# Segment 0's x turned by DMA transposes instead of TensorE, and half of wq on ScalarE's DMA queue

## The chip, the core and the metric

The kernel runs on one core of a Trainium2 chip. A core has TensorE (matmuls, output into PSUM), VectorE, ScalarE, GpSimd, SyncE (which here only issues DMAs) and 16 DMA engines. The engines run side by side, each through its own list of instructions in order, and wait for one another by semaphores. In the profile they are PE (PEld for TensorE's weight loads), DVE, ACT, POOL and SP. The metric is the device time of one execution in microseconds (us). The kernel before takes 264.84 us (median of 3 runs, 264.73 to 264.94).

## The reference

The input is x (2048 tokens by 512, bfloat16). Two branches read it, and a gate per token mixes them:

```python
g = sigmoid((x * gate_w).sum(-1, keepdims=True))
a = attention(x, wq, wk, wv, wo, beta)      # 32 heads of 16, 4 segments of 512 tokens
b = (relu(x @ W_gate) * (x @ W_up)) @ W_down  # inner width 1792
out = g * a + (1 - g) * b
```

In the attention each segment of 512 tokens has causal softmax attention within itself, and from segment 1 on a recall from a running memory `M` (16 x 16 a head) and normaliser `z` that sum phi(k) v and phi(k) over earlier segments; sigmoid(beta) mixes the two a head, and wo projects the result.

## The kernel before

**Tiling.** The work goes segment by segment (`NSEG = 4`, `L = 512` tokens). Every projection needs x with its features on the partitions: `xT[seg % 3]` is 128 x 4 x 512, block `ci` holding features 128 ci to 128 ci + 127 of the segment's 512 tokens. A projection of 128 outputs is four matmuls of 512 columns, one for each `ci`, summed in one of PSUM's 8 banks. Heads come in four groups (`c`) of eight; a group's q goes to `QT`, its k through `ktr` to `KT` with masks. Scores (`qk`, line 616, and `qk_diag`, line 629) fill four banks, ScalarE takes their exponent (line 638), and the values follow (`pv`, line 689). The FFN (`ffn_tasks`) runs over 14 inner tiles with `wg_sb` and `wu_sb`, then `wd_sb` and `wo_sb` for the output (`out_tile`).

**The order of the work.** Nothing is scheduled when the program is built: each piece is a task (`plan.add`) with an engine and dependencies, and the string `ORDER` lists all tasks by number in the order in which they are issued. `UNITS` gives each task its buffers. `LANDS` is the planner's estimate, in nanoseconds, of when each load arrives. Matmul tasks may run as one 128-column matmul (line 461) or as four 32-column ones (line 465), so that TensorE's array needs no change of mode; scores use it by rows, values by columns.

**The start.** All weights and segment 0's x are loaded at the start, from SyncE's queue but for three loads from ScalarE's (lines 300 to 327). Segment 0's x is loaded as it stands, tokens on the partitions, into `xn`, in four pieces: columns 0 to 255 of tokens 0 to 255 (`n0`, SyncE) and 256 to 511 (`n1`, ScalarE), then columns 256 to 511 likewise (`n2`, `n3`). Between them go wq's first two row blocks (`q0`, `q1`), after them wq's other half (`qb`), wk in two halves, wv, and the first pieces of the FFN weights. Meanwhile TensorE heats (`heat`, line 904): seven matmuls on constants, six of 512 columns and one of 384. Then `x0_tasks` turns x by matmuls against an identity (`flip`, line 498): 16 of 128 columns, two to a PSUM bank, each pair copied to `xT[0]` by VectorE (tokens 0 to 255) or ScalarE (256 to 511) (line 511). After the first eight turns a matmul on zeros (`junk`, line 505) fills the wait for the copies. Four projections by `wq` come between the first and the second eight turns. `proj_q` for segment 0 takes `ci` 0 and 1 as tasks of their own, and `ci` 2 and 3 as a third.

The same `xn` serves the token gate: `gate_tasks` multiplies it with `gwb` on VectorE (line 415) and sums. `xT` of segments 1 to 3 is not turned by TensorE: a DMA transpose brings each from x (`load_xT`, line 273); phi(k) is turned by DMA transposes too (`pK`, line 581). A DMA reports to its semaphore once from each of the 16 DMA engines, and has landed with the sixteenth report; the trace records the time of each report, and the text calls them its reports or landing records. Loads share eight semaphores in turn.

Of the kernel before, what the change touches and what calls it, by code (L numbers as in the profile page):

```python
# [12 lines left out]
P = 128  # L13
S = 2048
D = 512
# [15 lines left out]
    0 1 2 3 4 5 6 7 8 9 10 11 12 13 14 15 16 17 18 19 20 21 22 23 24 27 28 30 32 29 34 31 33 35  # L31
    36 83 57 70 84 37 43 41 39 38 58 44 96 42 40 97 71 59 85 60 98 61 86 62 99 74 63 87 72 64
    67 75 66 65 88 73 123 76 109 124 112 68 110 78 214 77 113 111 80 215 125 89 114 126 217 216
    81 220 127 91 218 47 115 116 90 46 223 93 129 128 219 25 224 130 221 117 238 26 239 226 222
    132 240 227 229 133 131 225 230 118 92 94 119 244 79 228 45 135 120 419 134 231 136 245 420
    48 241 121 242 421 49 416 122 246 147 243 365 50 148 137 232 346 55 233 69 51 138 366 53
    235 367 234 82 417 52 150 368 371 139 369 54 677 418 151 140 141 236 149 247 142 360 95 237
    152 153 361 143 154 248 56 362 256 250 249 257 144 363 350 100 258 156 145 251 157 259 364
    425 372 260 426 349 252 101 373 427 167 158 261 253 168 102 422 155 374 146 423 103 375 104
    106 424 262 169 170 376 159 171 107 263 160 161 108 254 347 393 264 172 255 173 377 394 174  # L40
    162 265 379 395 268 348 266 399 269 163 175 267 176 270 286 164 105 177 280 400 380 378 281
    401 388 381 389 282 178 179 385 390 289 180 271 382 384 287 397 165 283 284 370 166 290 288
    285 391 194 191 195 291 272 192 274 181 275 193 292 276 197 398 351 183 182 198 184 196 273
    293 185 295 186 296 352 294 199 200 354 356 187 407 297 201 357 550 188 408 396 189 551 402
    409 552 403 202 190 413 203 430 355 404 277 204 278 358 412 411 298 414 1008 299 556 431
    279 405 205 449 310 432 450 415 544 545 392 311 410 312 386 557 546 300 558 433 452 387 383
    206 353 453 406 207 434 301 208 451 302 209 313 454 455 210 696 456 428 303 314 429 304 359
    305 211 212 440 697 457 458 441 213 315 316 459 698 306 747 699 700 748 701 307 702 749 460
    461 317 308 462 753 703 318 309 750 704 751 754 463 752 474 755 334 475 335 464 336 756 319
    337 320 476 477 465 478 321 757 467 338 322 466 758 479 339 468 480 323 481 469 324 691 470  # L50
    471 692 325 472 553 482 693 483 340 484 559 326 554 341 555 694 560 485 495 561 327 547 496
    695 548 328 549 586 329 497 498 486 499 330 488 331 587 332 487 588 500 501 333 489 435 568
    502 436 569 490 437 342 571 491 572 438 570 492 504 439 607 503 573 505 608 493 580 343 583
    344 581 506 507 582 345 584 442 508 604 585 605 443 589 574 575 606 510 523 576 520 509 524
    590 609 577 591 578 511 521 579 525 526 512 513 527 562 522 592 514 563 610 515 564 528 529
    611 530 516 595 517 613 614 518 593 612 596 531 594 532 615 565 533 597 601 622 623 566 624
    598 534 567 599 625 600 780 535 781 602 537 616 617 603 536 618 782 783 538 619 784 626 759
    620 539 627 875 1072 760 876 540 621 785 444 877 1069 446 1073 445 1070 881 1074 1071 1075
    448 705 1076 447 706 1077 494 676 786 519 710 707 787 711 473 1027 541 1028 640 712 708 641
    788 542 642 716 882 1029 789 883 709 628 790 1022 1030 629 1032 714 1066 715 713 630 717  # L60
    1023 792 543 631 718 791 1024 793 1067 643 679 644 680 632 1025 633 1068 805 645 646 806
    795 647 794 634 1031 635 681 648 719 678 649 1026 808 796 809 650 807 636 637 798 651 797
    682 638 724 683 810 799 811 685 652 812 687 639 800 738 684 688 653 654 739 655 740 813 814
    725 815 686 741 656 742 726 664 689 657 743 720 727 665 729 744 728 658 721 816 730 905 745
    722 666 906 731 826 746 907 908 827 690 909 723 878 732 667 801 910 879 668 802 659 828 880
    829 817 803 830 887 819 888 660 818 889 831 669 820 832 893 833 821 670 822 894 823 661 824
    733 895 671 834 662 734 835 663 735 896 836 897 672 898 673 890 674 736 891 837 838 892 675
    929 839 930 737 911 920 912 931 884 840 913 885 841 921 854 886 761 932 855 762 933 763 917
    918 934 842 919 764 856 857 765 844 766 899 858 922 900 914 767 843 768 915 901 859 845 860
    902 916 861 903 771 769 923 846 904 924 772 944 847 770 925 848 953 863 862 849 926 864 941  # L70
    927 942 928 945 943 954 865 935 946 955 1099 866 1100 947 868 938 936 774 939 937 773 1101
    1102 867 940 1103 956 869 957 950 1079 1197 958 1104 775 870 948 776 1198 949 777 951 1199
    1038 804 1060 952 1191 779 1192 1061 778 1193 1055 871 1062 1007 1105 1039 850 1106 1033
    1065 1063 1034 1064 825 1056 1040 1203 1035 1204 1107 1108 1057 1205 1044 1043 1109 971
    1041 872 959 972 1042 873 960 961 1058 1078 973 1111 1036 874 962 1059 1112 963 974 1012
    964 965 1009 975 1114 1124 966 1011 1125 976 977 1037 978 979 1010 1045 1113 1127 851 1013
    1128 1046 1110 967 852 980 1126 968 981 1115 1014 1047 1129 1116 969 1016 1130 1117 982 983
    970 1131 1015 995 1018 1118 996 1019 984 1048 985 997 1049 1119 1132 1017 998 853 1133 1050
    1134 1206 1051 1020 999 1000 986 1054 1052 987 1053 1135 1145 1001 1146 1200 1021 1207 1120
    1121 1201 1002 1208 988 1147 1122 1148 1136 1149 1202 1003 1138 1004 1137 1005 989 1150  # L80
    1139 1151 1006 1080 1194 1152 1140 1221 1081 1141 1082 1209 1222 1142 990 1223 1154 1083
    1143 1153 1195 1084 1155 991 1196 1224 992 1210 993 1227 1156 1211 1157 994 1225 1158 1218
    1226 1090 1219 1228 1091 1212 1229 1230 1159 1170 1160 1085 1213 1171 1086 1231 1214 1215
    1216 1232 1239 1087 1217 1172 1173 1161 1174 1220 1240 1163 1162 1233 1088 1164 1234 1089
    1241 1175 1176 1165 1235 1236 1166 1177 1242 1167 1245 1168 1254 1246 1243 1178 1247 1179
    1092 1244 1237 1180 1093 1255 1238 1248 1249 1251 1250 1252 1181 1272 1253 1094 1182 1256
    1257 1095 1269 1184 1258 1263 1123 1259 1270 1096 1260 1271 1097 1183 1144 1266 1169 1267
    1185 1261 1275 1098 1287 1186 1273 1262 1276 1187 1274 1288 1264 1188 1289 1277 1265 1189
    1278 1279 1268 1290 1190 1280 1281 1291 1282 1292 1283 1293 1284 1294 1285 1295 1296 1286
    1299 1297 1300 1301 1302 1298 1311 1303 1304 1312 1305 1306 1313 1307 1314 1308 1315 1316  # L90
    1309 1317 1318 1319 1320 1310 1323 1324 1321 1325 1326 1327 1328 1329 1330 1331 1322 1334
    1335 1332 1336 1337 1338 1339 1333 1340 1341 1342 1343 1344 1345
"""

UNITS = (
    "456701230123437651300021111002224122032230000012000000020011000002000020000230111030011120"
    "02103432331105303722061118021a012d110b2039301c00111200112003013223002101312012022210110456"
    "1032000002200000002201100000130000000011011212202203031001930232127312532362238322b0014110"
    "a302d010c120110013221000110013220033101123323302145670321000002000000003301100000300003000"
    "0110113221211520132222122820302037110911243226210a120b320d302c0012120132321221212000322713"  # L100
    "30013456023100000230000000320110000020000000070011100311223231313002182225002410263107323a"
    "0119007c314d122b10011200110"
)


class Slot:


    def __init__(self, cands):
        self.cands, self.units, self.left = tuple(cands), (), 0  # L110

    @property
# [66 lines left out]
def kernel(  # L179
# [74 lines left out]
    def work():  # L254
        return plan.one("ps", range(7, -1, -1))


    LANDS = dict(n0=3700, n1=3750, n2=6000, n3=6050, q0=4950, q1=4950, qb=6800, ka=7900, kb=9300,
                 v=11500, g0=13000, u0=14000, gw=14800, be=15100, g1=16300, u1=17500, x1=20700,
                 g2=22000, u2=23100, g3=24200, u3=25300, d0=28100, d1=30800, o=33600)  # L260

# [708 lines left out]
```

## Time and profile before

| what | value |
|---|---|
| median of 3 runs | 264.84 us (264.73 to 264.94) |
| the profiled execution | 264.77 us |
| its span, first to last instruction | 263.1 us |
| TensorE (PE) busy | 259.0 us, 98% |
| VectorE (DVE) busy | 205.0 us, 78% |
| ScalarE (ACT) busy | 184.2 us, 70% |
| GpSimd (POOL) busy | 63.3 us, 24% |
| share of the DMA engines' time, queue 1 (SyncE) and queue 10 (ScalarE) | 25.3%, 0.5% |

Times in the profile are us from the span's start. A timeline line has the start, the duration of the group, the engine (`SPq` is SyncE's instruction queue issuing a DMA), the line of the kernel, the operation, what it writes and reads, and how many; in square brackets the engine's idle time before it and what ended it. A line of the waits has who waited for whom, the total in us, how often, and the longest. A line of the chain has start, duration and what ran: it is followed back from the last instruction to what released each step. A line of the windows has the stretch, its length, each engine's busy time in it, TensorE's granted clock, the DMA engines' busy share and GB/s. The clock column reads 1.00 throughout this trace, also where the spacing of the matmuls shows half speed; the text goes by the spacing. A busy TensorE includes the pipeline's latency, so the distance from one matmul's start to the next tells more than the busy share.

### The profile page before, as it was taken

The page shows a single profiled execution, that of the slowest core. Times are in us where ns is not written, and L with a number is a line of the kernel's source. Part 1 is how long each engine was busy: PE and PEld are TensorE (multiplying, and loading weights), DVE is VectorE, ACT ScalarE, POOL GpSimd, SP SyncE. Part 2 cuts the span into 40 slices and gives each one's busy share as a digit, 9 for nine tenths or more (in the row PEclk, how much of TensorE's full clock was granted, in tenths as well). Part 3 has the DMA queues.
Part 4 walks back from the last instruction along what each step waited for, and adds up shares of the span by engine and source line. Part 5 has one row for each costly group of instructions (what it writes and reads, how often), then busy time and mean ns, then how long its engine had stood idle before and what let it go on. Part 6 is the DMA issues. An engine that isn't in the chain of part 4 may idle for free.

```text
span 263.1 us, 8894 instructions
## 1 busy us (share of the span) xinstructions
PE 259.0 (98%) x3854; PEld 118.6 (45%) x3854; DVE 205.0 (78%) x474; ACT 184.2 (70%) x170; POOL 63.3 (24%) x168
## 2 busy tenths in 40 slices
PE   8999999999999999999999999999999999999995
PEld 3444434454444454544444444444444444445454
DVE  2899999899985666856999778794998887868622
ACT  3299988999777678887675877778487667892000
POOL 8022623223321323132012222032131223121000
DMA  6999892100822001200210120023020200320011
GB/s 199 328 273 346 231 187 42 24 2 18 132 82 60 2 22 36 79 2 2 80 22 22 36 42 21 22 75 110 0 82 1 57 5 30 102 73 22 2 42 42
DMA packets 30526, 19.46 MB, mean 74 GB/s; under 512 B 15000, under 2 KB 28952, under 8 KB 30488
## 3 DMA queue, kind: packets, MB, share of 16 engines
q1 hardware_dynamic: 29800, 18.51, 25.3%
q8 instruction: 30, 0.49, 0.8%
q10 hardware_dynamic: 688, 0.39, 0.5%
q14 instruction: 8, 0.07, 0.1%
HBM read 13.21 MB, written 2.55 MB: 60 GB/s over the span
## 4 chain that ended last, share of the span: by engine, by line
PE 92%; DVE 6%; issue 0%; DVEq 0%
PE ps L461 52%; PE ps L465 21%; PE ps L616 8%; PE ps L689 7%; PE ps L904 1%; PE ps L629 1%; DVE QT L549 1%; DVE KT L568 1%; DVE ktr L565 1%; PE ps L809 1%; DVE gcat L392 1%; PE ps L498 1%; PE ps L745 1%; DVE junk L415 0%; DVE hT L859 0%
## 5 line engine op out<-in xcount | busy, mean ns | idle before, releaser
L638 ACT ACTIVATE E<-ps 128x2048 bf16<-128x2048 f32 x64 | 120.1, 1877 | 33.2 <-PE ps L616 25.0
L667 POOL TENSOR_SCALAR_AFFINE_SELECT E<-E 128x256 bf16<-128x256 bf16 x128 | 54.0, 447 | 169.2 <-ACT E L638 169.2
L859 DVE TENSOR_TENSOR hT<-ps,rgr 128x512 bf16<-128x512 f32 x56 | 37.8, 680 | 15.0 <-PE ps L461 10.3
L853 ACT ACTIVATE rgr<-ps 128x512 bf16<-128x512 f32 x56 | 33.0, 597 | 15.7 <-PE ps L461 8.7
L461 PE MATMUL ps<-xT,wu_sb 128*128 128x512 bf16 x162 | 43.8, 380 | 0.0
L461 PE MATMUL ps<-wd_sb,hT 128*128 128x512 bf16 (+1 forms) x176 | 40.7, 354 | 0.0
L461 PE MATMUL ps<-xT,wg_sb 128*128 128x512 bf16 x146 | 40.1, 380 | 0.0
L720 DVE STREAM_TRANSPOSE T<-ps 128x512 f32<-128x512 f32 x32 | 22.4, 708 | 9.5 <-PE ps L689 9.2
L616 PE MATMUL ps<-QT,KT 32*128 32x320 bf16 (+3 forms) x512 | 25.4, 273 | 0.0
L461 PEld LDWEIGHTS <-wu_sb 128*128 128x128 bf16 x162 | 14.6, 98 | 18.1 <-issue 2.7
L461 PEld LDWEIGHTS <-hT 128*128 128x128 bf16 x176 | 15.0, 98 | 17.0 <-issue 2.7
L885 DVE TENSOR_SCALAR osr<-ps,ngcol 128x512 bf16<-128x512 f32 (+2 forms) x18 | 12.3, 687 | 12.6 <-PE ps L465 8.5
L461 PEld LDWEIGHTS <-wg_sb 128*128 128x128 bf16 x146 | 13.7, 98 | 16.9 <-issue 1.3
L465 PE MATMUL ps<-xT,wg_sb 128*32 128x512 bf16 x312 | 20.3, 379 | 0.0
L689 PE MATMUL ps<-E,Vp 128*17 128x320 bf16 (+3 forms) x512 | 19.4, 273 | 0.0
L616 PEld LDWEIGHTS <-KT 32*128 32x128 bf16 x512 | 7.6, 92 | 24.9 <-issue 22.5
L465 PE MATMUL ps<-wd_sb,hT 128*32 128x512 bf16 (+1 forms) x304 | 17.5, 359 | 0.0
L461 PE MATMUL ps<-xT,wq_sb 128*128 128x512 bf16 x62 | 17.5, 391 | 0.0
L461 PE MATMUL ps<-wv_sb,xT 128*128 128x512 bf16 x62 | 17.0, 379 | 0.0
L638 ACT ACTIVATE Em<-ps 128x2048 bf16<-128x2048 f32 x8 | 15.0, 1876 | 2.6 <-PE ps L629 2.6
L465 PE MATMUL ps<-xT,wu_sb 128*32 128x512 bf16 x248 | 16.7, 379 | 0.0
L461 PE MATMUL ps<-xT,wk_sb 128*128 128x512 bf16 x60 | 16.6, 380 | 0.0
(102 smaller groups left out, 301.0 us busy)
## 6 DMA issues: line engine op xcount, KB each, us to landing
out_dram<-osr SPq DMA_DIRECT2D x15, 128.0 KB
wd_sb<-in_B_W_down_dram SPq DMA_DIRECT2D x2, 896.0 KB
xn<-in_A_x_dram SPq DMA_DIRECT2D x3, 512.0 KB
cdr<-coefs SPq DMA_DIRECT2D x6, 256.0 KB
xn<-coefs SPq DMA_DIRECT2D x6, 256.0 KB
wg_sb<-in_B_W_gate_dram SPq DMA_DIRECT2D x2, 512.0 KB
wu_sb<-in_B_W_up_dram SPq DMA_DIRECT2D x2, 512.0 KB
wg_sb<-in_B_W_gate_dram SPq DMA_DIRECT2D x2, 384.0 KB
```

What stands on the lines that cost most here:

```text
L392: nc.vector.tensor_copy(gcat[rows, 0, c], g[rows, 0, c, (m + c) % 4])
L461: nc.tensor.matmul(out, lhsT=lhsT, rhs=rhs, start=start, stop=stop)
L465: nc.tensor.matmul(out[r], lhsT=lhsT[:, r], rhs=rhs, start=start, stop=stop, tile_position=(0, 32 * j))
L498: nc.tensor.matmul(bank(sl)[:, k * P:(k + 1) * P], lhsT=xn[:, 2 * t + k, ci * P:(ci + 1) * P], rhs=ident[:], start=True, stop=True)
L616: nc.tensor.matmul(ps[:, j * L + o:j * L + o + L - q], lhsT=KT[i][rows, kb, 3 * r:3 * r + 2].rearrange("p h q -> p (h q)"), rhs=QT[i][rows ...
L638: last_exp[0] = [plan.add("ACT", 66 + 4 * L / 1.2, key, lambda: nc.scalar.activation(dst, ps[:, 0:4 * L], ACT.Exp, scale=SCALE), [a] + war ...
L667: nc.gpsimd.affine_select(out=m[:, :, o:o + HP], in_=m[:, :, o:o + HP], compare_op=ALU.is_ge, fill=0.0, base=HP, pattern=[[0, 4], [1, HP]] ...
L689: nc.tensor.matmul(bank(sl)[32 * m:32 * m + HW, q:q + w], lhsT=(Vp[i] if n < 4 else Vm)[:, kb, r, 4 * c + j, 0:HW], rhs=rhs, start=(n == 0 ...
L720: done.append(plan.add("DVE", 633, key - RL, lambda r=r, sl=sl: nc.vector.transpose(T[ts.i][:, r], bank(sl)), [a] + done, 75 if r else 0, ...
L853: r = plan.add("ACT", 478, key - RL, lambda sl=gsl, rs=rs: nc.scalar.activation(rgr[rs.i][:], bank(sl), ACT.Relu), [g], ACL, frees=[gsl])
L859: nc.vector.tensor_tensor(hT[hs1.i][:], bank(sl), rgr[rs.i][:], ALU.mult)),
L885: nc.vector.tensor_scalar(osr[os.i][:, n0 - c0:n1 - c0], bank(sl)[:, 0:n1 - n0], ngcol[:, tt:tt + 1], None, ALU.mult)),
```

## The change

Segment 0's x is turned by TensorE for its first 128 columns only: two loads (`n0`, `n1`) bring those, 64 KB each instead of 128, four turns and one copy on VectorE and one on ScalarE follow. Two DMA transposes on SyncE's queue, in its third and fourth place, bring the other three blocks of `xT[0]` straight from x: one of 128 columns (`xb`), one of 256 (`x0`). wq's second half (`qb`) goes to ScalarE's queue, as its third load. Since `xn` still serves the token gate, its other 384 columns are loaded later, after the second pieces of the FFN weights and before segment 1's transpose (`n2`). The heating loses its last matmul of 384 columns; the filler on zeros becomes two of 256 columns. `LANDS`, `ORDER` and `UNITS` are new throughout: the order of all tasks of the program is another one.

```diff
-    LANDS = dict(n0=3700, n1=3750, n2=6000, n3=6050, q0=4950, q1=4950, qb=6800, ka=7900, kb=9300,
+    LANDS = dict(n0=3360, n1=3400, q0=4450, q1=4650, xb=5300, x0=6500, qb=6700, ka=7900, kb=9300,
...
-    got_n[0] = [load_x0(eng, 0, t) for t, eng in enumerate((nc.sync, nc.scalar))]
+    first, rest = slice(0, P), slice(P, D)
+    got_n[0] = [load_x0(eng, 2 * t, 2 * t + 2, first, "n%d" % t)
+                for t, eng in enumerate((nc.sync, nc.scalar))]
     got_q = [load(eng, wq_sb[:, ci, :], A_wq[ci * P:(ci + 1) * P, :], "q%d" % ci)
              for ci, eng in enumerate((nc.sync, nc.scalar))]
-    got_n[0] += [load_x0(eng, 1, t) for t, eng in enumerate((nc.sync, nc.scalar))]
-    got_q.append(load_rows(nc.sync, wq_sb, A_wq, 1, "q"))
+    got_x0b = []
+    for a, b, n in ((1, 2, "xb"), (2, NC, "x0")):
+        nc.sync.dma_start_transpose(out=xT[0][:, a:b, :], in_=x[0:L, a * P:b * P])
+        got_x0b.append(arrival(n))
+    got_q.append(load_rows(nc.scalar, wq_sb, A_wq, 1, "q"))
...
     load_gu(1)
+    got_n[0].append(load_x0(nc.sync, 0, NC, rest, "n2"))
     load_xT(1)
...
     def x0_tasks():
         got = []
-        for ci in range(NC):
-            for t in range(2):
+        for t in range(2):
...
+        def idle():
+            for k in range(2):
+                nc.tensor.matmul(bank(js)[:, 0:2 * P], lhsT=junk[:, 0:P],
+                                 rhs=junk[:, None, 0:P].to_broadcast([P, 2, P]), start=True,
+                                 stop=True)
+        j = plan.add("PE", 428, K(-9) + 2, idle, [a], lat=0, need=[js], frees=[js], size=4)
+        x0_first.extend([got + [(j, 0.0)], [got_x0b[0]]])
+        return [got + [got_x0b[0]], [got_x0b[1]]]
...
-        for k in range(7):
-            w = L if k < 6 else 3 * P
-            nc.tensor.matmul(bank(warm[k])[:, 0:w], lhsT=one.to_broadcast([P, P]),
-                             rhs=one.to_broadcast([P, w]), start=True, stop=True)
-    plan.add("PE", 3680, -1e9, heat, lat=0, need=warm, frees=warm, size=14)
+        for k in range(6):
+            nc.tensor.matmul(bank(warm[k])[:, :], lhsT=one.to_broadcast([P, P]),
+                             rhs=one.to_broadcast([P, L]), start=True, stop=True)
+    plan.add("PE", 3360, -1e9, heat, lat=0, need=warm, frees=warm, size=12)
```

In the changed program TensorE's list begins with the six heating matmuls, four turns, two fillers and sixteen projections by wq, the last two of them behind two by wk. The fifth of the sixteen waits for `xb`, the seventh for `x0` and `qb`.

## The prediction

> **What bounds the kernel now.** I read the page's busy shares and its chain, then the timeline of TensorE's first 9 us, since the change is made there.
>
> ```profile
> PE 259.0 (98%) x3854; PEld 118.6 (45%) x3854; DVE 205.0 (78%) x474; ACT 184.2 (70%) x170; POOL 63.3 (24%) x168
> PE 92%; DVE 6%; issue 0%; DVEq 0%
> ```
>
> TensorE is busy for 98% of the span and is 92% of the chain. So a change of other engines' work counts only where TensorE waits for it, and TensorE's own work counts in full. The timeline of TensorE:
>
> ```profile
> 0.84 3.04 PE L904 MATMUL ps<-const-bfloat16-1.0 128*128 128x512 bf16 x7 [0.84 <-PEq L954]
> 3.68 1.06 PE L498 MATMUL ps<-ident,xn 128*128 128x128 bf16 x8
> 4.53 0.42 PE L505 MATMUL ps<-junk 128*128 128x256 bf16 x1
> 4.77 1.66 PE L461 MATMUL ps<-xT,wq_sb 128*128 128x512 bf16 x4
> 6.35 0.77 PE L498 MATMUL ps<-ident,xn 128*128 128x128 bf16 x8
> 6.96 2.32 PE L461 MATMUL ps<-xT,wq_sb 128*128 128x512 bf16 x10
> ```
>
> A 512-column matmul starts every 0.427 us before about 6.07 us and every 0.216 us after 6.96 us: the clock doubles between the fourth projection matmul (start 6.02) and the second set of turns. Those turns wait for x's second halves (starts 6.35 and 6.61, landing records 6.30 and 6.57). After 6.96 us every gap between matmuls is that of a change of array mode (0.12 to 0.14 us), save one, which the waits and the chain between 7 and 26 us show:
>
> ```profile
> PEld L629 <- DVE KT L568: 0.4, 1, 0.4
> ```
>
> ```profile
> 8.45 1.89 DVE QT L549 x3
> ...
> 24.03 0.44 DVE KT L568
> ```
>
> The first diagonal scores (line 629, start 23.90) stand 0.49 us longer than the later ones, because VectorE, which works nearly without a pause from 8.45 us on, finishes KT late. From 8 to 24 us the two engines are bound together, and both start with the projections.
>
> **TensorE's head.** The heating loses its 384-column matmul (0.32 us): first turn at 3.68 - 0.28 = 3.40, if x's first columns are there. Now their records end at 3.53 (SyncE) and 3.73 (ScalarE); half the bytes in the same places land about 0.3 us earlier, in time. Four turns at 0.107 end at 3.83, two junk matmuls at 4.26. ScalarE's copy starts 0.35 us after its pair's second turn starts (now 3.997 to 4.345): 3.72 + 0.35 = 4.07, lasts 0.37, and the projection starts 0.05 later, at 4.49 instead of 4.77. ScalarE's table load is over at 3.63, as now, because its third load issue stays a load issue. Three copies fewer on VectorE and three on ScalarE cost nothing and gain nothing else: both engines stand idle there. Four projection matmuls at 0.427, with the clock doubling at 6.07, bring the fifth to 6.13 (now 6.96) and the seventh to 6.56 (now 7.39). If nothing were late, that is 0.83 us.
>
> **The two DMA transposes.** In the changed order the fifth matmul waits for the one-block transpose, the seventh for the two-block one and wq's second half. No transpose of these sizes runs before; the rows nearest are SyncE's issues of one block out of SBUF and of four out of x:
>
> ```profile
> 38.31 1.19 SPq L581 DMA_TRANSPOSE pK<-pkT  x1
> ```
>
> ```profile
> 64.39 2.03 SPq L273 DMA_TRANSPOSE xT<-in_A_x_dram  x1
> ```
>
> ```profile
> 8.00:9.00 1.00, 1.00 (x6) 0.49 (x5) 0.55 (x1) 0.00 (x0) 0.00 (x0) 1.00 1.08 382
> 37.00:37.50 0.50, 0.50 (x4) 0.20 (x2) 0.40 (x2) 0.50 (x1) 0.00 (x0) 1.00 1.28 290
> 38.75:39.50 0.75, 0.75 (x8) 0.22 (x9) 0.75 (x4) 0.75 (x2) 0.71 (x2) 1.00 0.01 2
> 39.50:40.25 0.75, 0.75 (x11) 0.31 (x4) 0.75 (x2) 0.56 (x2) 0.75 (x3) 1.00 0.89 173
> ```
>
> (The last figure of a window is GB/s.) The single block moves its first byte 1.2 us after the issue starts and reports 2.47 us after it; four blocks took 4.04 (issue 34.59) and 5.06 us (64.39). So two blocks, issued third and fourth on SyncE's queue at 1.83 and 3.05, take 2.47 + (1.57 to 2.59)/3 = 3.0 to 3.3 us: the second reports at 6.05 to 6.35 on an idle queue. The queue is not idle: loads issued at 1.83 to 2.30 now have their 16 reports spread over 4.64 to 6.30, 4.85 to 6.57 and 5.41 to 7.07 us, so the last engine trails the first by 1.7 us. The lower end is 6.3 (no wait, gain 0.83), the upper end 6.35 + 1.7 = 8.05 (a loss of 0.7). I take 6.8, a third of that lag, since the transposes come after the moment at which the short loads before them, whose reports spread 0.6 us, are done. The seventh matmul then starts at 6.85: **-0.54 us**. Behind it on TensorE stand all other projections, and VectorE's and ScalarE's copies wait for them, so this shift is the whole program's. wq's second half, now on ScalarE's queue third, has the place of a load that reported at 6.57; with twice its bytes, 6.3 to 6.8, it hides behind the transpose. The first transpose must report by 6.13 and is due at 1.83 + 2.47 = 4.3, so even the full lag hides.
>
> The Trainium skill's page Advanced Engine Details and Errata, section X-Bar Transpose (TRN2), calls transposes as fast as regular DMAs, at about 90% of a copy. The windows above show 290 against 382 GB/s, 76%; by the page the 256 KB would take 0.2 us less and the sum would be 0.2 us lower.
>
> **What is behind them on SyncE.** Two transposes (1.2 + 1.5 us of issue) replace two loads (0.47 each), so wk, wv and the FFN weights are issued about 1.8 us later (wk at 4.6). They move their first bytes 1.15 us after issue (first load: 0.80, first packet 1.95), at 5.7, when the transposes' bytes end, so the bytes ahead of each are the same as now. Now wk reports at 7.75 and 8.48, wanted at 8.6 and 9.4; wv at 9.98, wanted past 11.5; the first wg and wu at 11.48 and 12.85, wanted near 13.7 and 14.1. These margins cover it; if wk came the full 1.8 us late, the wait would be 0.9 us. The postponed 384 KB of x lie behind the second pieces of wg and wu (reports to 16.7): near 18, plus lag 18.7. VectorE reaches its first gate product, by the present durations, 12.4 us after the seventh matmul, at 19.2. x's next segment then comes 1.1 us later, 19.6 instead of 18.5, wanted at 24; W_down and wo (27 to 32 us) are wanted at 64.
>
> **The rest of the order.** I counted TensorE's work in both programs: the same matmul columns but for the turns, and the same changes of mode (50 full to row, 49 back, 23 row to column, 22 back), which the trace prices at 0.12 to 0.14 us each. So nothing changes there, except that the new order may or may not keep the 0.49 us at the first diagonal. Its VectorE list up to that KT holds the same operations less one of 0.2 us, but two more matmul pairs stand before the diagonal. Bounds: 0.49 gained, or 0.49 lost if another wait like it appears. I take **-0.25 us**. ScalarE (70%) and GpSimd (24%) keep their work.
>
> **Sum.** -0.54 - 0.25 = -0.79 us. The profiled execution took 264.77 us (span 263.1 and 1.7 around it), 0.07 below the median 264.84: 263.98 there, **264.1 us** against the median.
>
> **Rivals.**
> 1. *Everything lands in time and the diagonal's wait goes*: -0.83 - 0.49, 263.5 us. For it: idle-queue reports at 6.05 to 6.35. Against: every load of that stretch trailed.
> 2. *The second transpose reports at 7.5 to 8.0*: the head gains -0.1 to loses 0.6, less 0.25: 264.5 to 265.2, taken as no change. For it: the lag above. In four stretches of the trace transposed packets stalled about a microsecond while one engine lagged.
> 3. *The transposes hold SyncE up*: **slower**. x's transpose of segment 1 kept SyncE 7.02 us:
>
> ```profile
> 9.51 7.02 SPq L273 DMA_TRANSPOSE xT<-in_A_x_dram  x1
> ```
>
> If each early issue takes 0.8 us more, as one block behind a 512 KB load did (1.99 against 1.19), and the lag is kept, the second reports at 9.0: seventh matmul 9.05, +1.66 - 0.25, about 266.2 us. It decides from a report past 8.2. Against it: at 9.5 us over 2 MB were queued ahead, at 1.8 us 192 KB on that queue.
> 4. *The clock doubles later*: TensorE would stand idle 0.23 us (4.26 to 4.49), now 0.03. If the 5.2 us from the first matmul to the doubling had to start again at 4.49, the clock would stay low to 9.7; from 7.05 on only 6.2 matmuls fit instead of 13.2, 1.5 us lost: 265.6 us. No row shows such a restart. The Trainium skill's TensorE: Matmul & The Clock Gate, Part 1, lets a free-running window of about 3.4 us decide; one window more would mean 9.5 and 265.5 us.
> 5. *The new order waits elsewhere* (a gate product for the postponed x, or another KT) for over 1.3 us: 265.4 us or more.
>
> **How the numbers follow.** A change under 0.2% (0.53 us) can't be told from none here. Chances: forecast (263.7 to 264.3 and a little beyond) 0.38, rival 1 0.13, rival 2 0.2, rival 3 0.11, rival 4 0.08, rival 5 0.1. Faster: 0.38 + 0.13 = 0.51. Rival 2 gives 0.18 to no change and 0.02 to slower; slower is 0.31 in all. The likeliest case's own range is 263.6 to 264.5; the range 263.4 to 265.6 leaves out rival 3 and the worst of 5, and a little below rival 1.
>
> **What would show it.** Right: the seventh projection matmul at 6.6 to 7.0, waiting for the x DMA by no more than 0.4 us; 427 ns spacing ending near 6.1; SyncE's first transposes of 1.2 and 1.5 us; the first diagonal without its wait for KT; elsewhere mode changes alone. Wrong: a wait of over 1 us for xT on TensorE; SyncE held for over 2 us; 427 ns spacing past 7 us; VectorE waiting for xn near 19 us, or a long wait for wk.

## The result, and the profile after

The changed kernel takes 265.65 us (median of 8 runs, 264.62 to 265.77) against 264.88 us (8 runs, 264.08 to 265.29) for the kernel before, on the same chip: ratio 1.003, 95% interval 1.0016 to 1.0045. It is slower by 0.8 us (0.3%); the forecast was 264.1 us, and the range ended at 265.6. The profiled execution took 265.62 us, its span is 263.8 us against 263.1.

The busy shares and the chain of the page after:

```profile
PE 257.7 (98%) x3866; PEld 117.8 (45%) x3866; DVE 204.0 (77%) x471; ACT 183.6 (70%) x167; POOL 63.9 (24%) x168
PE 86%; DMA 5%; DVE 4%; SPq 4%; issue 1%; DVEq 0%
```

TensorE's share of the chain fell from 92 to 86%, and DMA and SyncE's queue (SPq), absent from the chain before, now make 9%: something waits for loads. TensorE's start, from its timeline after (start, duration, what ran, how many; in brackets the idle time before and what ended it):

```profile
0.84 2.72 PE L906 MATMUL ps<-const-bfloat16-1.0 128*128 128x512 bf16 x6 [0.84 <-PEq L956]
3.35 0.56 PE L501 MATMUL ps<-ident,xn 128*128 128x128 bf16 x4
3.75 0.38 PE L515 MATMUL ps<-junk 128*128 128x256 bf16 x2
4.52 1.74 PE L465 MATMUL ps<-xT,wq_sb 128*128 128x512 bf16 x6 [0.39 <-DVE xT L507]
6.66 1.89 PE L465 MATMUL ps<-xT,wq_sb 128*128 128x512 bf16 x8 [0.41 <-DMA xT<-in_A_x_dram]
8.88 0.61 PE L465 MATMUL ps<-xT,wk_sb 128*128 128x512 bf16 x2 [0.33 <-DMA wk_sb<-in_A_wk_dram]
```

The seventh projection starts at 6.66 us instead of 7.39: 0.73 us gained. But the eight matmuls from there end their turn at 8.39, and the first matmul by `wk`, the fifteenth projection in both kernels, starts only at 8.88, when `wk`'s first half has landed (8.83 us; 7.75 before). Before it started at 9.12. So 0.24 us of the 0.73 is left there. The first diagonal scores keep 0.21 us of their extra 0.49 (0.56 us from the first one to the next full matmul, 0.35 for the later ones): 0.28 us gained.

The loss stands at 41 us. TensorE's and VectorE's waits between 34 and 46 us, then VectorE's timeline, after:

```profile
DVE junk L419 <- DMA xn<-in_A_x_dram: 1.5, 1, 1.5
PE ps L465 <- DVE hT L862: 1.1, 1, 1.1
```

```profile
37.07 0.18 DVE L733 TENSOR_TENSOR cfr<-cfr,grc 128x32 f32<-128x32 f32 x1
38.74 0.69 DVE L419 SCALAR_TENSOR_TENSOR junk<-xn,gwb 128x512 bf16<-128x512 bf16 x1 [1.49 <-DMA xn<-in_A_x_dram]
...
39.47 0.77 DVE L419 SCALAR_TENSOR_TENSOR junk<-xn,gwb 128x512 bf16<-128x512 bf16 x1
...
40.17 0.88 DVE L728 TENSOR_TENSOR och<-T,cfr 128x512 bf16<-128x512 f32 x1
40.97 0.68 DVE L862 TENSOR_TENSOR hT<-ps,rgr 128x512 bf16<-128x512 f32 x1
```

VectorE's timeline before, at the same product:

```profile
35.49 0.18 DVE L730 TENSOR_TENSOR cfr<-cfr,grc 128x32 f32<-128x32 f32 x1
35.59 0.69 DVE L415 SCALAR_TENSOR_TENSOR junk<-xn,gwb 128x512 bf16<-128x512 bf16 x1
```

After, VectorE stands 1.49 us for segment 1's `xn`, which the gate product (line 419) reads; before, it goes on without a pause. Behind that product and a second one, in VectorE's order, stand two operations that TensorE needs; the `hT` (line 862) frees the bank for the matmul by `wg` at 41.70. The matmul ahead of that one starts 1.44 us earlier, where 0.22 us is the distance elsewhere: 1.23 us lost. The three together, -0.24 - 0.28 + 1.23 = +0.71 us, make up nearly all of the 0.76 us between the spans (263.83 and 263.07).

Why `xn` is late is in SyncE's timeline (issue start, time that the issue took). After, then before:

```profile
30.20 0.32 SPq L329 DMA_DIRECT2D wo_sb<-in_A_wo_dram  x1
33.70 1.35 SPq L584 DMA_TRANSPOSE pK<-pkT  x1
35.16 0.51 SPq L276 DMA_DIRECT2D xn<-in_A_x_dram  x1
```

```profile
27.36 0.32 SPq L325 DMA_DIRECT2D wo_sb<-in_A_wo_dram  x1
30.82 0.39 SPq L276 DMA_DIRECT2D xn<-in_A_x_dram  x1
31.25 3.30 SPq L581 DMA_TRANSPOSE pK<-pkT  x2
```

Loads share eight semaphores, so the eighth issue behind W_down's second half waits for that half: it reported at 33.62 (30.73 before). Before, that issue is `xn` itself, at 30.82. In the changed order it is the `pK` transpose, at 33.70, and `xn` stands behind it: issued 4.34 us later than before, landed at 38.72 instead of 35.15. W_down's 2.9 us of lateness had built up on the queue: 1.1 at `wk`, 1.7 at the second piece of `wu`, 2.7 at segment 1's transpose (22.75 against 20.09), behind the postponed 384 KB of x.

### The profile page after: what moved, and what is told of

Same layout as the page of the kernel before. It is cut to its first block, busy times and chain, and to the rows that moved or that the text cites. A ratio compares the mean times of both kernels' runs of the same rounds, so it can differ in the third digit from the quotient of the medians.

```text
span 263.8 us, 8916 instructions
## 1 busy us (share of the span) xinstructions
PE 257.7 (98%) x3866; PEld 117.8 (45%) x3866; DVE 204.0 (77%) x471; ACT 183.6 (70%) x167; POOL 63.9 (24%) x168
## 4 chain that ended last, share of the span: by engine, by line
PE 86%; DMA 5%; DVE 4%; SPq 4%; issue 1%; DVEq 0%
PE ps L465 48%; PE ps L469 21%; PE ps L692 7%; PE ps L619 7%; DMA xn<-in_A_x_dram 5%; SPq L266 2%; SPq L306 1%; PE ps L632 1%; DVE junk L419 1%; PE ps L812 1%; DVE gcat L396 1%; DVE T L723 1%; SPq L312 0%; DVE hT L862 0%; DVE KT L571 0%
## 5 line engine op out<-in xcount | busy, mean ns | idle before, releaser
L465 PE MATMUL ps<-xT,wu_sb 128*128 128x512 bf16 x176 | 48.5, 380 | 0.0
L465 PE MATMUL ps<-xT,wg_sb 128*128 128x512 bf16 x160 | 44.0, 380 | 1.1 <-DVE hT L862 1.1
L465 PE MATMUL ps<-wd_sb,hT 128*128 128x512 bf16 (+1 forms) x156 | 37.1, 351 | 0.0
L465 PEld LDWEIGHTS <-wu_sb 128*128 128x128 bf16 x176 | 16.3, 98 | 20.0 <-issue 1.9
L469 PE MATMUL ps<-wd_sb,hT 128*32 128x512 bf16 (+1 forms) x384 | 22.5, 364 | 0.0
L465 PEld LDWEIGHTS <-hT 128*128 128x128 bf16 x156 | 13.2, 98 | 15.2 <-issue 3.0
L469 PE MATMUL ps<-xT,wg_sb 128*32 128x512 bf16 x256 | 16.8, 379 | 0.0
L465 PE MATMUL ps<-wv_sb,xT 128*128 128x512 bf16 x54 | 15.1, 380 | 0.1
L465 PE MATMUL ps<-xT,wk_sb 128*128 128x512 bf16 x54 | 14.9, 379 | 0.3 <-DMA wk_sb<-in_A_wk_dram 0.3
L552 DVE CAST QT<-ps 128x512 bf16<-128x512 f32 x16 | 10.9, 684 | 4.9 <-PE ps L465 4.9
```

Source lines behind the costliest of these rows:

```text
L465: nc.tensor.matmul(out, lhsT=lhsT, rhs=rhs, start=start, stop=stop)
L469: nc.tensor.matmul(out[r], lhsT=lhsT[:, r], rhs=rhs, start=start, stop=stop, tile_position=(0, 32 * j))
L552: prj["q", seg, c] = plan.add("DVE", 600, key - RQK, lambda: nc.vector.tensor_copy(QT[i][:], bank(sl)), [a], DVL, frees=[sl])
```

## The experiments

Theory A: the loss is SyncE's list, `pK` ahead of `xn`, where both wait for a late W_down. Rivals: the lateness alone, which the postponed x and the transposes bring; or VectorE's own work. Times are medians, ratios are to the kernel before on the same chip with 95% intervals.

**e1_xn_first: the order alone.** In `ORDER`, task 335 (segment 1's `xn`) goes ahead of task 58 (`pK`):

```diff
-    ... 137 225 58 126 354 44 355 226 409 335 127 ...
+    ... 137 225 335 58 126 354 44 355 226 409 127 ...
```

> The changed kernel with one task moved in the order: on SyncE, segment 1's xn load is issued ahead of the phi(k) transpose (pK) instead of behind it. Theory A (the 1.23 us that TensorE waits for hT near 41 us come from SyncE's list: pK waits for the semaphore of W_down's late second half until 33.6, takes 1.35 us to issue, and xn stands behind it): xn is issued near 33.7 to 34.0 instead of 35.16, since its own semaphore's earlier load reports at about 33.9, and lands near 37.3 to 37.6 instead of 38.7; VectorE's wait for it falls from 1.5 us to 0.1 to 0.4, TensorE's to 0 to 0.2, and the time by 1.0 to 1.2 us: near 264.5, at or below the kernel before. Rival B (the wait would come from VectorE's own work or from somewhere else in the order): TensorE still stands 1 us or more near 41 us and the time stays within 0.3 us of the changed kernel's. Rival C (pK, now behind xn, becomes the late one): pK is issued near 35, 1.3 us later, and a matmul that takes phi(k) turned waits for it, so that 0.5 us or more of the gain is lost again.

Measured: 264.50 us (12 runs), ratio 0.9991 (0.9975 to 1.0006). SyncE's timeline, and two lines of TensorE's:

```profile
34.29 0.39 SPq L276 DMA_DIRECT2D xn<-in_A_x_dram  x1
34.72 3.85 SPq L584 DMA_TRANSPOSE pK<-pkT  x3
```

```profile
9.46 0.61 PE L465 MATMUL ps<-xT,wk_sb 128*128 128x512 bf16 x2 [0.78 <-DVE QT L552]
...
26.06 0.59 PE L465 MATMUL ps<-wv_sb,xT 128*128 128x512 bf16 x2 [0.53 <-DVE hT L862]
```

W_down came later still (34.19), yet `xn` was issued at 34.29 and no wait is left near 41 us, nor one for `pK` (rival C). The margin is small: `xn` landed at 37.96, and VectorE came to it at 38.12. The loss of 1.1 us against the changed kernel's 265.65 is gone, by one exchange in a list: Theory A, and rival B falls. The second fence shows what remains: here `wk` landed at 9.41 (the line names VectorE, but the matmul ran 0.05 us after the landing), and a new wait of 0.53 us near 26, which e6 and e11 take up.

**e2_before_pk_first: the same order in the kernel before.** Tasks 69 (`pK`) and 346 (`xn`) exchanged:

```diff
-    ... 148 137 232 346 55 233 69 51 138 ...
+    ... 148 137 232 69 346 55 233 51 138 ...
```

> The kernel before with one task moved in the order: the pK transpose is put ahead of segment 1's xn load on SyncE, as the changed kernel has it; all loads at the start are those of before. Theory A (order and lateness both needed): pK's issue ends near 32 (W_down's second half reports at 30.7, 1.2 to 1.35 us of issue), xn is issued near 32.1 to 32.3 instead of 30.82 and lands near 36.2 to 36.6 instead of 35.15; VectorE wanted it at 35.6, so it waits 0.6 to 1.0 us, TensorE 0.3 to 0.8, and the time rises by 0.3 to 0.8 us. Rival B (lateness of the loads alone does it; the order is harmless): TensorE has no new wait near 41 us and the time stays within 0.2 us of the kernel before.

Measured: 266.51 us (10 runs, 265.46 to 267.87), ratio 1.007 (1.0048 to 1.0092): 1.7 us, twice the most that was expected. The profiled execution was the longest; SyncE's timeline and the waits:

```profile
32.47 2.28 SPq L581 DMA_TRANSPOSE pK<-pkT  x1
34.85 0.51 SPq L276 DMA_DIRECT2D xn<-in_A_x_dram  x1
```

```profile
DVE junk L415 <- DMA xn<-in_A_x_dram: 3.4, 1, 3.4
PE ps L461 <- DVE hT L859: 2.9, 1, 2.9
```

Direction and mechanism as expected, the size not: W_down's second half reported at 32.39 in this execution, with the same loads in the same order that reported at 30.73 in the profile before, and the `pK` issue took 2.28 us. The place behind W_down exposes `xn` to how late W_down happens to be.

**e3_before_late: lateness alone.** The kernel before with 384 KB more in the place of the postponed load (into a buffer that is overwritten later):

```diff
     load_gu(1)
+    nc.sync.dma_start(out=xT[2][:, :, 0:3 * P],
+                      in_=x[0:L, P:D].rearrange("(t p) n -> p t n", p=P))
     load_xT(1)
```

> The kernel before with one more load of 384 KB on SyncE's queue (x's columns 128 to 511 of segment 0, into the buffer that segment 2's transpose overwrites later) in the place where the changed kernel has its postponed load of x. The order of the tasks is that of before, xn ahead of pK. Theory A: W_down's halves report about 1.0 to 1.1 us later (28.4 and 31.8 instead of 27.3 and 30.7), xn is issued near 31.9 and lands near 36.2; VectorE, which wanted it at 35.6, waits 0.4 to 0.7 us, TensorE 0 to 0.5; the time rises by 0 to 0.5 us. If lateness alone explained the whole loss (rival B), 1.1 us of lateness out of the changed kernel's 2.9 would cost near 1.1 us less the margin of 0.4, 0.7 us.

Measured: 264.70 us (12 runs), ratio 1.0004 (0.9991 to 1.0017). SyncE's timeline:

```profile
32.33 0.38 SPq L276 DMA_DIRECT2D xn<-in_A_x_dram  x1
32.76 2.86 SPq L583 DMA_TRANSPOSE pK<-pkT  x2
```

`xn` was issued 1.5 us later than before and landed at 35.89, and neither VectorE nor TensorE waited for it there: VectorE came to it at 35.96, 0.07 us after the landing. So a W_down that is 1.5 us late (32.24) costs nothing without the order, and rival B falls for that much. The 2.9 us of the changed kernel are more than e3 has; for those e1 speaks, where W_down was 3.5 us later than before and cost nothing near 41 us.

**e4_no_late_x and e13_no_late_x_again: the order without the postponed load.** The load of x's other columns is left out, GpSimd writes zeros there:

```diff
-    got_n[0].append(load_x0(nc.sync, 0, NC, rest, "n2"))
+    got_n[0].append(arrival("n2"))
...
+    nc.gpsimd.memset(xn[:, :, rest], 0.0)
```

> The changed kernel without its postponed load of x's other 384 columns: GpSimd fills them with zeros, so that segment 0's token gate is computed from the first 128 columns alone (this part of the computation is left out). Order and everything else as in the changed kernel. Theory A: all loads behind it come about 1.0 us earlier, W_down's second half reports near 32.6, pK and xn follow, xn lands near 37.6; VectorE's wait falls from 1.5 us to about 0.4 to 0.5 and TensorE's from 1.23 to 0.1 to 0.3: 0.9 to 1.1 us faster than the changed kernel. VectorE's small wait at 19.5 us goes too and is worth nothing on TensorE. Rival B (most of the lateness is not this load's but the transposes' at the start): W_down's second half moves by less than 0.5 us, and the time by less than 0.5 us.

Measured: 265.66 us (12 runs, 264.82 to 266.51), ratio 1.003 (1.0014 to 1.0045). By the median nothing was gained, against the expectation of 0.9 to 1.1 us; but the profiled execution was the shortest, with W_down's second half at 32.19, `xn` landed at 37.72 and no TensorE wait at 41. So the same kernel was traced again:

> The kernel of e4_no_late_x once more (x's postponed 384 columns left out, zeros in their place; pK ahead of xn), for a second profile: the first one fell on the shortest of twelve executions (264.82 of 264.82 to 266.51) and shows no TensorE wait near 41 us, while the median is 1.1 us above that of e7_no_late_x_xn_first, which differs only in the place of pK. Theory A (W_down's second half often lands later than the 32.2 us of that profile, and pK ahead of xn turns each such microsecond into a wait for xn): a profiled execution near the median, 265.4 to 266.0, has W_down's second half at 33 or later, xn landing past 38.3, VectorE waiting 1.0 us or more for it and TensorE 0.7 to 1.2 us for hT. Rival B (something else in that order costs 0.8 us in most executions): at a time near 265.7 TensorE's wait for hT near 41 us is under 0.4 us, and a wait of that size is elsewhere. If the profiled execution is again one near 264.8, this stays open.

Measured: 265.22 us (10 runs, 264.77 to 266.53), ratio 1.0011 (0.9997 to 1.0026). This profile fell on the longest execution. SyncE's timeline and the waits near 41 us:

```profile
33.28 1.21 SPq L585 DMA_TRANSPOSE pK<-pkT  x1
34.67 0.44 SPq L276 DMA_DIRECT2D xn<-in_A_x_dram  x1
```

```profile
DVE junk L420 <- DMA xn<-in_A_x_dram: 1.9, 1, 1.9
PE ps L466 <- DVE hT L863: 1.3, 1, 1.3
```

W_down's second half at 33.20, `xn` at 38.97: the two profiles of one kernel, 1.0 us apart at W_down, are 1.7 us apart in time, and 1.32 us of that arise across this wait (the rest is near 109 us and at the head, see the account below). So between these two profiles the time goes with W_down's landing. The 22 runs of both have a median of 265.4.

**e6_after_again and e7_no_late_x_xn_first: the two by two.** The changed kernel as it is, and e4 with e1's exchange.

> The changed kernel as it is, once more, on the same chip as the other runs of this call. Theory A (loads behind pK, stall of TensorE for hT near 41 us): 265.4 to 265.8, 0.8 to 1.2 us slower than e5 and e8 and 0.6 to 1.0 slower than the kernel before, with VectorE waiting 1.0 to 2.0 us for xn near 38 us. If the stall depended on a chance state of the first profile alone (rival B), this profile would show less than 0.5 us there.

> The changed kernel with both edits of e1_xn_first and e4_no_late_x: xn ahead of pK, and no postponed load of x's other 384 columns (zeros in their place, so segment 0's token gate is computed from the first 128 columns alone). e4 by itself did not get faster on the median (265.66 against 265.65). Theory A (the order on SyncE is the cause, the postponed load is only 1 us of a lateness that the right order hides): within 0.2 us of e1_xn_first, 264.3 to 264.7. Rival B (the postponed load costs something by itself, through VectorE's wait near 19.5 us or the loads behind it): 0.3 us or more faster than e1_xn_first.

| | `pK` ahead of `xn` | `xn` ahead of `pK` |
|---|---|---|
| changed kernel | 265.65 and 265.77 (e6) | 264.50 (e1) |
| without the postponed load | 265.66 (e4) and 265.22 (e13) | 264.57 (e7) |
| kernel before | 266.51 (e2) | 264.88 |

Ratios: e6 1.0032 (1.0015 to 1.0049), e7 0.9995 (0.9983 to 1.0007). Each row has 0.7 to 1.7 us between its columns (e13's interval alone overlaps e7's, e4's does not); down the second column nothing can be told apart. e6 shows the stall again, SyncE's timeline and the waits:

```profile
33.44 1.21 SPq L584 DMA_TRANSPOSE pK<-pkT  x1
34.76 0.51 SPq L276 DMA_DIRECT2D xn<-in_A_x_dram  x1
```

```profile
DVE junk L419 <- DMA xn<-in_A_x_dram: 1.4, 1, 1.4
PE ps L465 <- DVE hT L862: 1.0, 1, 1.0
```

It also has the wait of 0.53 us near 26 that e1 had. Its chain between 8 and 27 us (start, duration, what ran):

```profile
10.94 8.48 DMA xn<-in_A_x_dram
...
19.45 0.70 DVE junk L419 x2
...
24.72 0.60 DVE hT L862
25.32 0.04 issue
25.37 0.38 PE ps L465
```

Here the postponed x (landed 19.42, in e1 20.07) starts VectorE's gate product, and the `hT` behind it keeps TensorE. VectorE stands only 0.12 us for it, though (0.07 in e1, 0.04 in the changed kernel's first profile). Another 0.20 is the `KT` copy just ahead of the `hT`: 0.48 us in e6 and 0.49 in e1, where GpSimd's operation on `E` (line 670) runs beside nearly all of it, and 0.28 in the changed kernel's first profile and in e7, where that operation begins later. In all these traces no `KT` copy without it takes over 0.36 us. No run tested whether the one slows the other. That the postponed x costs time on the median is not shown: e7, without that load, is no faster than e1.

**e5_wq_before_wk, e8_wk_on_scalar, e9_wq0_on_scalar: the head.** All three start from e1. e5 puts two more matmuls by `wq` ahead of the first two by `wk` (task 48 ahead of 50); e8 puts `wk`'s first half on ScalarE's queue; e9 puts `wq`'s first row block there, so that the transposes are issued 0.5 us earlier:

```diff
-    ... 88 47 50 75 48 51 ...
+    ... 88 47 48 50 75 51 ...
```

```diff
-    got_k = [load_rows(nc.sync, wk_sb, A_wk, i, "k") for i in range(2)]
+    got_k = [load_rows((nc.scalar, nc.sync)[i], wk_sb, A_wk, i, "k") for i in range(2)]
```

```diff
-             for ci, eng in enumerate((nc.sync, nc.scalar))]
+             for ci, eng in enumerate((nc.scalar, nc.scalar))]
```

> The kernel of e1_xn_first (changed kernel, xn ahead of pK) with one more task moved: the last pair of matmuls by wq is put ahead of the first pair by wk, so that TensorE has 0.43 us of work more before it needs wk. Theory A (the head's gain is given back because wk lands 0.5 to 1 us later than before: the first matmul by wk starts at 8.9 to 9.5 in the three kernels with transposes traced so far and at 9.0 to 9.5 in the three without, though the seventh projection starts 0.5 us earlier on the mean): the first matmul by wk starts after wk has landed with a wait shorter by 0.43 us, everything behind it comes up to 0.43 us earlier, and the time falls by 0.2 to 0.43 us against e1_xn_first, to 264.1 to 264.3. Rival B (VectorE's chain from the first wk matmul to the first scores is what counts there): the first scores start at the same time after wk and the time stays within 0.15 us of e1_xn_first's.

> The kernel of e1_xn_first with wk's first half on ScalarE's queue, as its fourth load, instead of on SyncE's behind the two transposes: it is issued at 2.35 us instead of 4.43. Theory A (wk is late because SyncE's transposes take 2.5 us to issue): wk's first half reports by 7.5, TensorE's wait for it (0.5 and 0.95 us in the two profiles) goes, and if its 256 KB do not delay the second transpose the time falls by 0.4 to 0.6 us against e1_xn_first. Rival B (the DMA engines are the limit, and wk's bytes then go ahead of the transposes'): the second transpose reports at 7.2 to 7.6 instead of 6.6 to 6.75, the seventh projection starts 0.5 to 0.8 us later, the first matmul by wk no earlier than 9.0, and the time is within 0.3 us of e1_xn_first. ScalarE's table load comes 0.5 us later (ends near 4.1 instead of 3.63) and may hold its copy and the first projection by 0.1 us.

> The kernel of e1_xn_first with wq's first row block on ScalarE's queue as its second load (wq's other two loads behind it there), so that SyncE's two transposes come second and third, 0.5 us earlier. Theory A (the transposes and wk are late because of their place in SyncE's list): the first transpose is issued at 1.3, the second at 2.6, wk at 3.9; the second transpose reports 0.3 to 0.5 us earlier than the 6.6 to 7.5 of the profiles so far (mean 7.0), the first matmul by wk starts 0.3 to 0.5 us earlier than the 9.0 of their mean, and the time is 0.3 to 0.5 us below e1_xn_first's. Rival B (the DMA engines' own pace sets the landing): the second transpose still reports near 7.0 and the time stays within 0.2 us. ScalarE's table load ends 0.5 us later, near 4.1, and costs its copy at most 0.1 us.

Measured: e5 264.85 us, ratio 0.9993 (0.9979 to 1.0007); e8 265.57, 1.0025 (1.0007 to 1.0042); e9 264.80, 0.9997 (0.9984 to 1.0010). TensorE's timelines of e8 and of e9, at the wait for the transposes:

```profile
7.53 2.58 PE L465 MATMUL ps<-xT,wq_sb 128*128 128x512 bf16 x10 [1.07 <-DMA xT<-in_A_x_dram]
```

```profile
7.53 1.89 PE L465 MATMUL ps<-xT,wq_sb 128*128 128x512 bf16 x8 [1.02 <-DMA xT<-in_A_x_dram]
```

In e8 `wk`'s first half landed at 7.44, as wanted, but the first transpose came at 7.49 and the second at 8.19 (5.62 and 6.62 in the changed kernel), and it is 1.1 us slower than e1 (0.9 by the ratios): the 256 KB on ScalarE's queue landed ahead of both transposes, which came 1.4 to 1.6 us later than e1's. In e9 the transposes were issued at 1.32 and 2.60 instead of 1.83 and 3.10, and the second still reported at 7.48; in e12 below, which has e9's head, it reported at 6.97. At the later place it reported at 6.60 to 7.48. So the earlier place on SyncE shows no earlier landing (rival B, which e8 exceeded); that the DMA engines' load sets it is likely from e8 and not shown by e9. The Trainium skill's page DMA: Bandwidth & Descriptors, section Queues, rings and completion order, says that SyncE's and ScalarE's queues are rings on the same 16 DMA engines, not engines of their own; e8 agrees. e5 gained nothing on the median. Its profile can't tell why: the second transpose came at 7.48, and TensorE reached `wk` after it had landed.

**e11_x_rest_earlier and e12_all_edits: a better version.** e11 is e1 with the postponed load ahead of the second pieces of `wg` and `wu`:

```diff
+    nc.sync.dma_start(out=xn[:, :, rest], in_=x[0:L, rest].rearrange("(t p) n -> p t n", p=P))
     load_gu(1)
-    got_n[0].append(load_x0(nc.sync, 0, NC, rest, "n2"))
+    got_n[0].append(arrival("n2"))
```

e12 is e11 with the edits of e5 and e9.

> The kernel of e1_xn_first with the postponed load of x's other 384 columns one place earlier, ahead of the second pieces of wg and wu instead of behind them. Theory A (in two of the profiles with the new order, e1_xn_first and e6_after_again, VectorE's first gate product starts only when that load lands, at 20.07 and 19.42 us, and a TensorE wait of 0.53 us for hT follows near 26): the load lands near 16.5 to 17.5, that wait goes, the second pieces land 1.0 us later, near 18.5 and 19.8, ahead of their use past 20.5, and the time falls by 0.1 to 0.4 us, the half of 0.53 on the mean. Rival B (VectorE is about as late by its own work): within 0.1 us. Rival C (the second pieces come too late): a wait for wg or wu near 21 to 23, and slower.

> All four edits together on the changed kernel: xn ahead of pK, the last pair of wq matmuls ahead of the first pair by wk, wq's first row block on ScalarE's queue, the postponed x ahead of the second pieces of wg and wu. By Theory A of each, added: 263.6 to 264.2, 0.3 to 0.9 us below e1_xn_first and 0.7 to 1.2 below the kernel before. If only the order on SyncE near 33 us mattered (rival B), 264.4 to 264.7.

Measured: e11 264.43 us (12 runs), ratio 0.9978 (0.9965 to 0.9990); e12 264.74, 0.9989 (0.9978 to 1.0000). e11 beats both kernels, the one before by 0.5 us. In its profile the postponed x landed at 16.66, the second pieces at 18.08 and 19.51, and no wait is near 26 us or for `wg` or `wu`; 0.36 us are left near 41, where VectorE stood 0.69 us for `xn` (W_down 33.71, `xn` landed 37.38). So with `xn` ahead of `pK` a late W_down can still cost something. Against e1 it is 0.07 us by the medians and 0.0013 by the ratios, within their intervals, so the gain from the moved load itself is not shown. e12's sum of gains did not come: of its four edits the two at the head had brought nothing alone.

**The account over all profiles.** The profiles of the new order differ by 2.2 us (262.42 to 264.59), and the difference can be followed to four places. The head first: the time of the seventh and the fifteenth projection, which is the first by `wk` (in e5, where it is another one, the time of its place), in the profiles whose first loads are those of the kernel before or of the changed kernel.

| | x's last part reports | seventh projection | fifteenth projection |
|---|---|---|---|
| before, e2, e3 | 6.57, 6.41, 6.94 | 7.39, 7.23, 7.76 | 9.12, 8.96, 9.49 |
| after, e1, e4, e5 | 6.62, 6.75, 7.31, 7.48 | 6.66, 6.79, 7.35, 7.52 | 8.88, 9.46, 9.08, 9.25 |
| e6, e7, e11, e13 | 6.96, 7.05, 6.60, 6.92 | 7.00, 7.09, 6.64, 6.97 | 8.73, 8.81, 8.48, 8.69 |

The means are 7.46 and 7.00 us for the seventh, 9.19 and 8.92 for the fifteenth: of 0.46 us gained, 0.27 is left where `wk` is needed.

A place that no theory had named came out of what was left over: near 109 us, between the sixth and the seventh of a row of sixteen short matmuls on `Em`, TensorE stands for up to 0.76 us, and nothing that the profile shows ends it ("issue"). TensorE's timelines of e13 and of e7 there:

```profile
110.43 0.22 PE L693 MATMUL ps<-Em,Vm 128*17 128x64 bf16 x6
111.22 0.26 PE L693 MATMUL ps<-Em,Vm 128*17 128x64 bf16 x10 [0.57 <-issue]
```

```profile
108.93 0.39 PE L693 MATMUL ps<-Em,Vm 128*17 128x64 bf16 x16
```

The trace's packets of the instruction queue, q8, show a 16 KB fetch a little ahead of it in every profile, of 0.88 to 1.43 us. In all eleven profiles with the changed order or a variant of it the seventh of these matmuls starts 1.34 to 1.56 us after that fetch's end, whether the gap is 0.03 us (e1) or 0.76 (e13); the three with the order of before have no such gap. So the wait goes with the fetch of instructions. No run tested that; it would take another program layout.

With it the account closes. The starts of ScalarE's exponents (one for each four banks of scores) stand at the same distances, to 0.01 us, in all profiles of one order but for the waits, so the waits are read from what those distances are too long: of the first five distances for the waits before 29 us, of the tenth and eleventh for that near 41. The last column is the span less the four numbers ahead of it in the row.

| | fifteenth projection | waits near 15 and 26 | wait near 41 (`xn`) | gap near 109 | span | rest |
|---|---|---|---|---|---|---|
| after | 8.88 | 0.13 | 1.23 | 0.15 | 263.83 | 253.44 |
| e6 (the same) | 8.73 | 0.56 | 1.13 | 0.73 | 264.59 | 253.44 |
| e13 | 8.69 | 0.20 | 1.43 | 0.76 | 264.58 | 253.50 |
| e4 | 9.08 | 0 | 0.11 | 0.29 | 262.96 | 253.48 |
| e1 | 9.46 | 0.51 | 0 | 0.03 | 263.45 | 253.45 |
| e7 | 8.81 | 0 | 0 | 0.10 | 262.42 | 253.51 |
| e11 | 8.48 | 0 | 0.36 | 0.25 | 262.53 | 253.44 |
| before | 9.12 | none | 0 | none | 263.07 | 253.95 |
| e3 | 9.49 | none | 0 | none | 263.37 | 253.88 |
| e2 | 8.96 | none | 3.25 | none | 266.16 | 253.95 |

The waits near 26 (0.13 us in the changed kernel's first profile, 0.5 in e1 and e6) stand in the three profiles in which VectorE waited for the postponed x; the 0.20 of e13 and 0.05 in e6 are for the first piece of `wu`, near 15. The rest is constant within 0.07 us in either order, and the new order's is 0.5 us shorter. 0.42 of that is the first diagonal: it stands 0.07 to 0.08 us longer than the later ones in e4, e7 and e11, against 0.49 before.

## Why the prediction was wrong

**TensorE's head** came as worked out to the first projection: first turn at 3.35 (forecast 3.40, which takes off 0.28 of the 0.32 us of the lost matmul; all of it gives 3.36), first projection at 4.52 (4.49). The clock's doubling, forecast at 6.07, was at 3.7 in this profile, and little followed from it, since the projections waited for the transposes instead.

**The two transposes**: issues of 1.22 and 1.29 us (1.2 and 1.5), the second reported at 6.62, 6.96 on the mean of eight (6.8); seventh projection 6.66, on the mean 7.00 (6.85). The gain of 0.54 us measured 0.73 in the profile, 0.46 on the means. Right in mechanism and size. The first transpose was 1.3 us later than due (5.62 for 4.3), within the lag allowed. wq's half (5.09, forecast 6.3 to 6.8) hid as said.

**What is behind them on SyncE** is the step that failed, at two of its statements. First, "these margins cover it": `wk` was given 0.85 us of margin (7.75, wanted at 8.6). It came 1.08 us later, at 8.83, and TensorE wanted it at 8.39, since the head had gained 0.73 and not 0.54. That took 0.49 of the 0.73 us back, 0.19 of 0.46 on the means. It is a term of the sum set at nothing. Second, and it decides the sign, "W_down and wo (27 to 32 us) are wanted at 64". That is when TensorE reads them. An earlier one is SyncE itself: the eighth issue behind W_down's second half takes over its semaphore. That issue was the `pK` transpose, with `xn` behind it, wanted by VectorE at 37.3. The step asked who uses the data, and not which instruction waits for the semaphore and what is queued behind it. The runs put 1.1 us on it (e1 against the changed kernel). e2 shows that the order does it in the other kernel too, and e3 and e1 that a W_down 1.5 and 3.5 us late is hidden where `xn` goes first; with `pK` first, W_down's landing sets how much is lost. A smaller slip: the 18.5 us given for segment 1's transpose is where its reports begin (18.40); the last came at 20.09, and after the change at 22.75, not 1.1 but 2.7 us later.

**The rest of the order** gave more than forecast: 0.5 us against 0.25, the best of its bounds (0.49), with the changes of mode at 0.12 to 0.14 us as said and the first diagonal's wait nearly gone where nothing else is late. But "so nothing changes there" held for TensorE's own list alone. The step compared the two orders on TensorE, ScalarE and VectorE, not on SyncE, where `pK` and `xn` had changed places; and the gap near 109 us, 0.34 us on the mean of the eleven profiles, was in no row of before.

**The rivals.** Rival 5, a new wait elsewhere of over 1.3 us at a chance of 0.1, is what came: 1.23 us in the profile, at a gate product, though for segment 1's x and not for the postponed one, which goes with 0.13 there and 0.5 in e6. Rivals 1 to 3 did not come; e5's report at 7.48 us is at the edge of rival 2. Rival 3's 9.0 us is not what its terms give: two issues 0.8 us longer each put 6.8 at 8.4, and with the whole lag 9.65. Rival 4 had no ground: the projections waited for the transposes whenever the clock doubled. In e7 matmuls still started 0.42 us apart up to 5.84 us, and the seventh started at 7.09, 0.04 after its transpose reported.

So the terms of the sum, on the means: head -0.27 for -0.54, order -0.5 for -0.25, together near the -0.79 of the forecast; then +0.34 for the instruction gap, some +0.1 to 0.5 near 26 us, beside the postponed x, and +1.1 to 1.2 for `xn`, none of which was in it. Without the last, e1 and e7 stand at 264.50 and 264.57, 0.3 us below their kernel before, with intervals that include no change.

## What to carry to other kernels

When a change reorders a DMA queue, follow the queue's own list: for each issue, which earlier load its semaphore belongs to, and what is queued behind it and for whom; a load may have 30 us of slack for its data and none for its semaphore. An issue that must wait for a big load belongs behind the small load that an engine needs soon, not ahead of it. A gain at the start of the program is worth what is left of it at the next load that does not move with it.

## What was not expected of the hardware

The same loads in the same order land at very different times from execution to execution. W_down's second half: 30.73 us in the profile before and 32.39 in e2; 33.62 and 33.36 in the two profiles of the changed kernel, 32.19 and 33.20 in the two of e4's. An order without margin there spreads with it (264.8 to 266.5 us for e4 and e13, 265.5 to 267.9 for e2).

TensorE's clock doubled, by the spacing of its matmuls, at times at least 2.1 us apart, with the same matmuls ahead of it: near 3.7 us in the changed kernel's first profile (turns 0.107 us apart, then 0.074 to the next matmul), and not before 5.8 in e7 (projections 0.42 us apart up to 5.84, the next pair 0.215). The Trainium skill's TensorE: Matmul & The Clock Gate, Part 1, has a free-running window decide, and a transition that varies by 0.5 us either way; the first agrees with these profiles, the second is too narrow for them.

A transpose's landing did not follow its issue: 0.5 us earlier on SyncE left the second one at 7.48 us in e9 and at 6.97 in e12, against 6.60 to 7.48 at the later place. What in the DMA engines holds it is not settled by these runs.

TensorE can wait for its own instructions in the middle of a row of short matmuls: 0.03 to 0.76 us near 109 us in eleven profiles, always ending 1.34 to 1.56 us after the end of a 16 KB packet on the instruction queue.
